# The first batch's v as casting transfers from GpSimd's queue, one per head

## The chip, the cores and the metric

One core of a Trainium2 chip runs the program. Its engines run side by side, each through its own list of instructions in order, and wait for one another by semaphores: TensorE (PE: matmuls and transposes, with PEld its weight loads), VectorE (DVE), ScalarE (ACT), GpSimd (POOL) and SyncE (SP), which here only issues transfers. Transfers issued by SP and by GpSimd travel in two queues and are carried by the same 16 DMA engines. The metric is the device time of one execution in microseconds (us). What is compared is the median over runs of the kernel before and of the changed kernel.

## What is computed

Two blocks, one behind the other, in f32. The first is a linear attention with a decaying state, for 4 batches, 8 heads, 768 positions and 64 columns a head:

```python
for t in range(S):
    state = gamma[None, :, None, None] * state + np.einsum('bhd,bhe->bhde', k[:, :, t], v[:, :, t])
    y[:, :, t] = scale * np.einsum('bhd,bhde->bhe', q[:, :, t], state)
```

Its heads are laid side by side into x, 768 x 512 for each batch. The second block mixes x by the real part of a two-dimensional Fourier transform, normalises and adds a two-layer network (512 to 2048 to 512):

```python
X = np.fft.fft(np.fft.fft(x, axis=1), axis=2)
u = x + np.real(X)
un = (u - mean) / np.sqrt(var + 1e-06)
out = u + np.maximum(un @ w_ch1, 0.0) @ w_ch2
```

## The kernel before, in words

**Tiling.** The 768 positions are six chunks of 128. Heads are handled in pairs, four pairs a batch in the order 0, 1, 3, 2 (`PAIR_ORDER`); "pair 0 to 3" below means the place in that order. For each pair q, k and v come from memory as f32 tiles of 128 partitions x 768 values (384 KB). GpSimd turns them into f16: q (L398), k times its decay, one instruction per head (L407, L410), and v (L423). TensorE transposes q and k by chunks (L439), ScalarE copies the transposes out of PSUM (L447, L450), TensorE multiplies k by q within a chunk (L464, the scores) and k by v (L486, the states' increments), VectorE masks the scores (L471) and scans over the chunks (L495), and TensorE makes y from both: scores by v (L510), q by states (L526). ScalarE scales y into x (L539).

**Stages.** The first batch's attention runs by itself at the start (`first_units`), together with the building of the sine and cosine tables (L288 to L292 on VectorE, L316 to L325 and L301 on ScalarE). Then the network of batch b runs while the attention of batch b + 1 is woven into it. The first network matmuls of batch 0 are L953; those of the other parts are L936 and L979.

**Order.** In the first batch the order on every engine is written out by hand: `first_units` makes a list of small functions, each emits its instructions, and `pin` ties every instruction to the one before it on the same engine. So the place of a unit in that list is the place of its instructions in each engine's own list. `filler(n)` puts n matmuls without use (L151) on TensorE at such a place.

**Loads.** All twelve loads of the first batch are issued by SP at the start, L165, in the order q, k, v of pair 0, then of pair 1, and so on. They go into the pool `inp`, which has 11 buffers. GpSimd issues the eight transfers of the network's weights (w1: L993, w2: L1000), which change f32 into f16 on the way; the first of them stands between the q cast and the k cast of pair 3. The loads of batch 1, on SP again, wait for the seventh weight transfer and for a matmul of L953.

**What the change touches.** `load_unit` for batch 0 (L158 to L181), the v cast `v0_unit` (L418), and its places in `first_units` (L1054 to L1074). The casts `q0_unit` (L394) and `k0_unit` (L402) stand beside it on GpSimd and keep their form; for pair 3 the second k head is done by ScalarE (L414) and the second half of v by VectorE (L427). The f16 tile of v comes from the pool `vp`, which has four buffers. GpSimd's list through the first batch is: set-up; then q, k, k, v of pair 0; of pair 1; two small constants (L351, L353); of pair 2; then q, the first weight transfer, k, v of pair 3; then the other seven weight transfers.

Of the kernel before, what the change touches and what calls it, by code (L numbers as in the profile page):

```python
# [12 lines left out]
ALU = mybir.AluOpType  # L13
f32 = mybir.dt.float32
# [4 lines left out]
P = 128  # L19
B, H, S, D = 4, 8, 768, 64  # L20
DM = 512
DFF = 2048
NCH = S // P
# [6 lines left out]
PAIR_ORDER = [0, 1, 3, 2]  # L30
# [6 lines left out]
LD0, LD1 = (0.172, 0.226), (-0.370, 0.140)  # L37
HT0 = (0.655, 0.675, 0.673, 0.628)
NPE = 2
ACT_ROWS = ((2, 5, 6, 7, 8, 9, 10, 14), (0, 3, 6, 7, 9, 10, 11, 12, 14, 15), (2, 4, 5, 6, 7, 8, 10, 14))  # L40


@with_exitstack
def kernel(
# [113 lines left out]
    def load_unit(b, i, after=None):  # L158
        def run():
            h0 = 2 * PAIR_ORDER[i]  # L160
            for name, src in srcs.items():
                t = inp.tile([P, 2, NCH, D], f32, tag="in32", name=f"{name}32")
                rows = "h (p c) d -> p h c d" if b < NPE and name == "q" else \
                    "h (c p) d -> p h c d"
                dma = nc.sync.dma_start(t, src[b, h0:h0 + 2].rearrange(rows, p=P))  # L165
                if after is not None:
                    for x in (w_dma[after].ins, lb[0]["mm"].ins):
                        tc.add_manual_dep(dma.ins, x.name,
                                          mybir.DependencyInfo(mybir.DependencyClass.Sync,
                                                               mybir.DependencyReason.DATA),  # L170
                                          reason="loads in turn")
                if b > 1:
                    tc.add_manual_dep(dma.ins, a_of[b - 1, 1].ins.name,
                                      mybir.DependencyInfo(mybir.DependencyClass.Sync,
                                                           mybir.DependencyReason.DATA),
                                      reason="loads behind the transposes")
                in_of[name, b, i] = t
        return run

    for i in range(4):  # L180
        load_unit(0, i)()  # L181


    icol_i = const.tile([P, 8], i32, tag="icol_i")
# [44 lines left out]
    def gk_unit(hp):  # L229
        def run():  # L230
            nc.scalar.copy(gk5[:, hp, :, 1:], gk2[:, hp:hp + 1].unsqueeze(1).to_broadcast(
                [P, D, NCH - 2]))
        return run
# [62 lines left out]
    def ts_dve(c):  # L296
        return trig_dve(c, S, KN, icol[:, c:c + 1], icoln[:, c:c + 1])
# [10 lines left out]
    def t_act(idx, part):  # L308
        w = KN if idx < 3 else 257
        r = rs[2 * idx][:, 0:w]  # L310
        ra = rs[2 * idx + 1][:, 0:w]
        sc = float(2.0 * np.pi / (S if idx < 3 else DM))

        def run():
            if part == 0:
                nc.scalar.activation(ra, r, AF.Abs, bias=0.0, scale=1.0)  # L316
            elif idx < 3:
                src = (ra, r)[part - 1].rearrange("p (i t) -> p t i", t=2)
                dst = (csp, ssp)[part - 1]
                nc.scalar.activation(dst[:, :, idx, :], src, AF.Sin,  # L320
                                     bias=hpi if part == 1 else 0.0,
                                     scale=-sc if part == 1 else sc)
            else:
                src, dst = (ra, r)[part - 1], (cd16, sd16)[part - 1]
                nc.scalar.activation(dst[:, idx - 3, :], src, AF.Sin,  # L325
                                     bias=hpi if part == 1 else 0.0, scale=-sc)
        return run
# [89 lines left out]

    def v0_unit(i):  # L418
        def run():
            v32 = in_of.pop(("v", 0, i)).rearrange("p h c d -> p c h d")  # L420
            v16 = v16_of[0, i] = vp.tile([P, NCH, 2, D], f16, tag="v16", name="v16")
            n = NCH if i < 3 else 3
            last_cast[0, i] = nc.gpsimd.tensor_scalar(  # L423
                out=v16[:, 0:n], in0=v32[:, 0:n], scalar1=1.0, scalar2=1.0, op0=ALU.mult,
                op1=ALU.mult)
            if n < NCH:
                nc.vector.tensor_copy(v16[:, n:], v32[:, n:])  # L427
        return run

    def t0_unit(i, part):  # L430
# [84 lines left out]
    def yx_unit(i):  # L515
        def run():
            st = at[0, i]
            first = i == 3
            if first:
                for h2 in range(2):  # L520
                    st["y", h2] = ps_y.tile([P, NCH, D], f32, tag="y", name="wkY",
                                            padded_shape=[P, 8, D])
            for c in range(1, NCH):
                for h2 in range(2):
                    sl = slice(64 * h2, 64 * h2 + 64)
                    nc.tensor.matmul(st["y", h2][:, c, :], st["qT"][sl, c, :],  # L526
                                     st["s16"][sl, :, c - 1], start=first and c == 1,
                                     stop=not first and c == NCH - 1, skip_group_check=True)
        return run
# [507 lines left out]
    def first_units():  # L1037
        def a(i):
            un = [am_unit(i, 0), am_unit(i, 1)]
            return un  # L1040

        def e(i, *hh):
            return [ae_unit(i, half, h2) for half, h2 in hh]

        def y(i):
            return [yi_unit(i, 0), yi_unit(i, 1)]

        def x(i):
            return [x0_unit(i, 0), x0_unit(i, 1)]

        std = ((0, 0), (0, 1), (1, 0), (1, 1))
        heads = ((0, 0), (1, 0), (0, 1), (1, 1))
        o = PAIR_ORDER
        un = [ts_dve(0), gk_unit(o[0]), gk_unit(o[1]), t_act(0, 0), t_act(0, 1),  # L1054
              q0_unit(0), t0_unit(0, 0), filler(4), ts_dve(1), te_unit(0, 0), t_act(0, 2),
              k0_unit(0), t0_unit(0, 1), filler(3), te_unit(0, 1), ts_dve(2), td_dve(0), t_act(1, 0),
              t_act(1, 1), t_act(1, 2), v0_unit(0)]
        un += a(0) + [filler(1), kv0_unit(0)] + e(0, *std) + [sc_unit(0)]
        un += [q0_unit(1), t0_unit(1, 0), te_unit(1, 0), t_act(2, 0), t_act(2, 1), filler(4),
               k0_unit(1), t0_unit(1, 1), te_unit(1, 1)]  # L1060
        un += y(0) + [parity_consts, yx_unit(0), filler(2)] + x(0) + [t_act(2, 2), v0_unit(1),
                                                                     half_ids]
        un += a(1) + [csn_unit(0), filler(1), kv0_unit(1)] + e(1, *std) + [sc_unit(1)]
        un += [q0_unit(2), t0_unit(2, 0), te_unit(2, 0), csn_unit(1), filler(3), k0_unit(2),
               t0_unit(2, 1), te_unit(2, 1)]
        un += y(1) + [td_dve(1), yx_unit(1), filler(2)] + x(1) + [
            gk_unit(o[2]), t_act(3, 0), t_act(3, 1), v0_unit(2)]
        un += a(2) + [filler(1), kv0_unit(2)] + e(2, *std) + [sc_unit(2), t_act(3, 2),
                                                              csn_unit(2)]
        un += [q0_unit(3), w1_unit(0), t0_unit(3, 0), te_unit(3, 0), filler(3)] + y(2)  # L1070
        un += [fold_s(0, 0, 258, 0, 1), g0_unit(0, (0,)), k0_unit(3), t0_unit(3, 1),
               te_unit(3, 1), yx_unit(2), gk_unit(o[3]), x0_unit(2, 0), x0_unit(2, 1),
               t_act(4, 0), t_act(4, 1), filler(2), v0_unit(3)]
        un += [w1_unit(g) for g in range(1, 4)] + [w2_unit(g) for g in range(4)]  # L1074
        un += a(3) + e(3, (0, 0), (1, 0)) + [kv0_unit(3), filler(4), sc_unit(3), t_act(4, 2)]
        un += e(3, (0, 1), (1, 1))
        un += [yx_unit(3), yi_unit(3, 0), x0_unit(3, 0), filler(1), yi_unit(3, 1), x0_unit(3, 1),
               g0_unit(0, (1,)), filler(1)]
        un += [fold_s(0, 0, 130, 1, 2), fold_d(0, 0), s1_unit(0, 0, 0), fold_s(0, 130, 258, 1, 2),
               px_unit(0), fold_d(0, 1, (0,)), xmean_unit(0), fold_d(0, 1, (1,)),  # L1080
               s1_unit(0, 1, 0), s1_unit(0, 0, 1), s1_unit(0, 1, 1), g0_unit(0, (2,)),
               mean_unit(0)]
        un += [s2_unit(0, 0), px_unit(1), s2_unit(0, 1), norm_unit(0, 0), gr_unit(0), gr_unit(1),
               px_unit(2), filler(2), unT_unit(0, 0), xmean_unit(1), mean_unit(1),
               norm_unit(0, 1), s2_unit(0, 2), xmean_unit(2), mean_unit(2), norm_unit(0, 2),
               gr_unit(2), gr_unit(3), edge_zeros, x_edges(1)]
        return un
# [94 lines left out]
```

## Time and profile before

| What | Value |
|---|---|
| runs shown, median (lowest to highest) | 247.04 us (246.52 to 247.95), 3 runs |
| span of the profiled execution, first to last instruction | 245.4 us |
| busy share of the span: PE, PEld, DVE, ACT, POOL | 95%, 59%, 72%, 51%, 33% |
| bytes moved, mean rate | 36.39 MB, 148 GB/s |
| queue of SP: packets, MB | 94960, 31.86 |
| queue of GpSimd: packets, MB | 4224, 4.19 |

The profile gives one execution by its span; the runs' times are taken from outside it and are some 1.6 us longer. The issue of a transfer is an instruction of the queue that issues it; its landing is a later event. In the first batch these are, from the timeline of SP and the time from issue to landing of each load:

| Pair | q: issued, landed | k: issued, landed | v: issued, landed |
|---|---|---|---|
| 0 | 0.81, 4.1 | 1.32, 5.9 | 1.82, 7.6 |
| 1 | 2.69, 8.8 | 4.99, 10.6 | 5.50, 12.3 |
| 2 | 7.08, 13.5 | 9.61, 15.2 | 10.12, 16.9 |
| 3 | 11.66, 19.5 | 14.37, 21.3 | 14.95, 22.5 |

A line of a timeline reads: start in us, length in us, engine, line of the kernel, operation, tile written <- tiles read, shapes and types, count; in brackets the idle time of the engine just before, and the engine and line that ended it. Where several instructions are merged, the length is that of all of them. When several semaphores are waited for, the last one by the profile is named, which need not be the one that held.

### The profile page before, as it was taken

How to read it: one execution, taken by the hardware profiler on the slowest of the kernel's cores; microseconds unless marked ns; L12 is line 12 of the kernel's file. 1: busy time of each engine (PE TensorE's matmuls, PEld its weight loads, DVE VectorE, ACT ScalarE, POOL GpSimd, SP SyncE). 2: the span in 40 equal slices, each digit the busy share in tenths (PEclk: the TensorE clock that was granted, in tenths of full speed). 3: DMA queues.
4: the chain of work that ended last, by engine and by line, in shares of the span. 5: the costliest groups of instructions: out<-in, count | busy, mean ns of one | idle time of the engine just before them, and what ended most of it. 6: DMA issues, size and time to landing. Idle time of an engine off the chain costs nothing.

```text
span 245.4 us, 5309 instructions
## 1 busy us (share of the span) xinstructions
PE 234.2 (95%) x2024; PEld 143.8 (59%) x2024; DVE 177.0 (72%) x430; ACT 124.2 (51%) x276; POOL 81.7 (33%) x146
## 2 busy tenths in 40 slices
PE   6997899999999998999999999999999999999995
PEld 2454668956776655665567546655666455445543
DVE  8997957897897788996885748887895656424112
ACT  8798669587775434751247414742247317202500
POOL 6667601465600057690000646660002405000000
PEclk9999999999999999999999999999999999999999
DMA  8999999699999377999999667786200241221012
GB/s 173 256 260 140 204 195 205 164 245 230 291 229 222 75 168 165 191 181 137 256 272 214 116 141 203 129 120 139 87 1 0 45 151 21 47 85 43 0 45 85
DMA packets 99209, 36.39 MB, mean 148 GB/s; under 512 B 89840, under 2 KB 96240, under 8 KB 99184
## 3 DMA queue, kind: packets, MB, share of 16 engines
q1 hardware_dynamic: 94960, 31.86, 62.2%
q0 software_dynamic: 4224, 4.19, 10.7%
q8 instruction: 16, 0.26, 0.5%
q14 instruction: 9, 0.07, 0.1%
HBM read 27.26 MB, written 6.29 MB: 137 GB/s over the span
## 4 chain that ended last, share of the span: by engine, by line
PE 71%; DMA 7%; DVE 7%; POOL 4%; ACT 4%; SPq 3%; issue 1%; POOLq 0%; ACTq 0%; DVEq 0%
PE psc L979 30%; PE psh L936 25%; DMA k<-in_k_dram 5%; PE ps L736 3%; SPq L165 3%; PE wkA L600 3%; DMA q<-in_q_dram 2%; PE wkY L654 2%; PE pq L833 2%; PE wkY L650 1%; POOL u L870 1%; PE wkK L619 1%; ACT un L885 1%; DVE bst L889 1%; POOL kd L407 1%
## 5 line engine op out<-in xcount | busy, mean ns | idle before, releaser
L979 PE MATMUL psc<-w,ht 128*128 128x512 f16 (+2 forms) x400 | 89.3, 371 | 0.0
L936 PE MATMUL psh<-unT,w 128*128 128x384 f16 x448 | 81.6, 326 | 0.4 <-ACT ht L940 0.2
L979 PEld LDWEIGHTS <-ht 128*128 128x128 f16 x400 | 37.5, 98 | 36.5 <-issue 0.2
L936 PEld LDWEIGHTS <-w 128*128 128x128 f16 x448 | 42.3, 98 | 24.7 <-issue 1.4
L940 ACT ACTIVATE ht<-psh 128x384 f16<-128x384 f32 x64 | 30.9, 489 | 41.7 <-PE psh L936 41.1
L870 POOL TENSOR_TENSOR u<-u,x 128x256 f32<-128x256 f32 x21 | 13.3, 635 | 100.3 <-DVE u L840 91.0
L983 DVE SCALAR_TENSOR_TENSOR ob<-psc,stats,u 128x512 f32<-128x512 f32 (+2 forms) x25 | 18.1, 726 | 26.1 <-PE psc L979 26.0
L942 DVE TENSOR_SCALAR ht<-psh 128x384 f16<-128x384 f32 x48 | 26.2, 548 | 7.7 <-PE psh L936 7.4
L603 DVE TENSOR_TENSOR atm<-wkA,maskp 128x512 f16<-128x512 f32 x36 | 23.8, 681 | 1.6 <-PE wkA L600 1.6
L891 ACT ACTIVATE un<-u,stats 128x512 f16<-128x512 f32 x21 | 15.2, 722 | 16.7 <-DVE stats L890 12.1
L889 DVE BATCH_NORM_STATS2 bst<-u 128x6 f32<-128x512 f32 x21 | 14.6, 694 | 7.7 <-POOL u L872 7.6
L629 DVE SCALAR_TENSOR_TENSOR s<-s,gk,wkK 128x128 f16<-128x128 f16 x48 | 16.3, 341 | 3.7 <-ACT s L625 2.7
L662 ACT ACTIVATE x<-wkY,gexp 128x384 f16<-128x384 f32 x24 | 12.8, 581 | 8.0 <-PE wkY L654 8.0
L151 PE MATMUL wps<-ht 128*128 128x512 f16 x40 | 13.5, 444 | 2.2 <-POOL ht L202 2.2
L383 POOL TENSOR_SCALAR kd<-k,gexp 128x384 f16<-128x384 f32 x24 | 13.8, 585 | 3.6 <-DMA k<-in_k_dram 3.6
L872 POOL TENSOR_TENSOR u<-u,x 128x256 f32<-128x256 f32 x21 | 13.3, 635 | 3.0 <-DVE stats L890 3.0
L600 PE MATMUL wkA<-qTz,kT 128*128 128x256 f16 x72 | 13.4, 273 | 0.1
L835 ACT COPY qn<-pq 128x128 f32<-128x128 f32 x18 | 4.9, 272 | 13.6 <-PE pq L833 13.6
L953 PE MATMUL psh<-unT,w 128*128 128x128 f16 x192 | 11.5, 219 | 0.1
L953 PEld LDWEIGHTS <-w 128*128 128x128 f16 x192 | 11.0, 98 | 0.7 <-issue 0.5
L840 DVE SCALAR_TENSOR_TENSOR u<-pq,g,qn 128x256 f32<-128x256 f32 x18 | 8.5, 472 | 3.3 <-PE psh L936 2.5
L388 POOL TENSOR_SCALAR v<-v 128x768 f16<-128x768 f32 x12 | 10.0, 831 | 1.3 <-DMA v<-in_v_dram 1.3
(164 smaller groups left out, 315.6 us busy)
## 6 DMA issues: line engine op xcount, KB each, us to landing
q<-in_q_dram SPq DMA_DIRECT2D x16, 384.0 KB, 6.3
k<-in_k_dram SPq DMA_DIRECT2D x16, 384.0 KB, 5.6
v<-in_v_dram SPq DMA_DIRECT2D x16, 384.0 KB, 6.3
out_dram<-ob SPq DMA_DIRECT2D x23, 256.0 KB, 2.6
w<-in_moe_w_ch_dram POOLq DMA_DIRECT2D x8, 512.0 KB, 10.8
unT<-un SPq DMA_TRANSPOSE x15, 2.4
out_dram<-ob SPq DMA_DIRECT2D x1, 192.0 KB, 1.9
qTz<-q16z SPq DMA_TRANSPOSE x8, 3.9
```

Of the source, the lines that this page charges most:

```text
L600: mm = nc.tensor.matmul(wk[:, c2], st["kT"][:, c, :], st["qT"][:, :, c, :], start=True, stop=True)
L603: nc.vector.tensor_tensor(out=st["atm"][:, 2 * part:2 * part + 2], in0=wk, in1=maskp[:, PAIR_ORDER[i]].unsqueeze(1).to_broadcast([P, 2, 2, ...
L629: nc.vector.scalar_tensor_tensor(out=s16[:, c], in0=s16[:, c - 1], scalar=gk2[:, hp:hp + 1], in1=wk[:, c - c0], op0=ALU.mult, op1=ALU.add)
L870: nc.gpsimd.tensor_tensor(out=u[:, kb, 0:256], in0=u[:, kb, 0:256], in1=x[:, kb, 0, 1:257], op=ALU.add)
L889: nc.vector.bn_stats(bst, u[:, kb, :])
L891: una = nc.scalar.activation(un, u[:, kb, :], AF.Identity, bias=stats[:, kb, 0:1], scale=-1.0)
L936: nc.tensor.matmul(psh, w116[:, cb, fb * P:(fb + 1) * P], unT[:, cb, rt * 384:(rt + 1) * 384], start=(cb == 0), stop=(cb == 3))
L940: nc.scalar.activation(ht16[:, fb, :], psh, AF.Relu, bias=0.0, scale=-1.0)
L942: nc.vector.tensor_scalar(out=ht16[:, fb, :], in0=psh, scalar1=-1.0, scalar2=0.0, op0=ALU.mult, op1=ALU.max)
L953: mm = nc.tensor.matmul(psh[:, f], w116[:, cb, fb * P:(fb + 1) * P], unT[:, cb, kb * P:(kb + 1) * P], start=(cb == 0), stop=(cb == 3))
L979: nc.tensor.matmul(psc[:, c0:c1], ht16[:, fb, rb3 * P:(rb3 + 1) * P], w216[:, fb, c0:c1], start=(fb == 0), stop=(fb == NFB - 1))
L983: nc.vector.scalar_tensor_tensor(out=ob[:, c0:c1], in0=psc[:, c0:c1], scalar=lb[b]["st"][:, rb, 3:4], in1=lb[b]["u"][:, rb, c0:c1], op0=AL ...
```

## The change

Batch 0's v is no longer loaded by SP. SP issues eight loads for it, q and k of the four pairs. `v0_unit` no longer casts; it issues two transfers on GpSimd's queue, one per head, each of which reads f32 from memory and writes f16 into the tile of v directly. The unit also moves in the list: that of pair 0 to the very front, before the q cast of pair 0, and those of pairs 1, 2 and 3 to the places where those of pairs 0, 1 and 2 stood. The load and the casts of batches 1 to 3 stay as they were.

```diff
+HW0 = ("q", "k")
...
+    def load0(name, i):
+        h0 = 2 * PAIR_ORDER[i]
+        t = in_of[name, 0, i] = inp.tile([P, 2, NCH, D], f32, tag="in32", name=f"{name}32")
+        rows = "h (p c) d -> p h c d" if name == "q" else "h (c p) d -> p h c d"
+        nc.sync.dma_start(t, srcs[name][0, h0:h0 + 2].rearrange(rows, p=P))
+
     for i in range(4):
-        load_unit(0, i)()
+        for name in HW0:
+            load0(name, i)
...
     def v0_unit(i):
         def run():
-            v32 = in_of.pop(("v", 0, i)).rearrange("p h c d -> p c h d")
+            h0 = 2 * PAIR_ORDER[i]
             v16 = v16_of[0, i] = vp.tile([P, NCH, 2, D], f16, tag="v16", name="v16")
-            n = NCH if i < 3 else 3
-            last_cast[0, i] = nc.gpsimd.tensor_scalar(
-                out=v16[:, 0:n], in0=v32[:, 0:n], scalar1=1.0, scalar2=1.0, op0=ALU.mult,
-                op1=ALU.mult)
-            if n < NCH:
-                nc.vector.tensor_copy(v16[:, n:], v32[:, n:])
+            for h2 in range(2):
+                last_cast[0, i] = nc.gpsimd.dma_start(
+                    v16[:, :, h2, :], v[0, h0 + h2].rearrange("(c p) d -> p c d", p=P))
         return run
...
-        un = [ts_dve(0), gk_unit(o[0]), gk_unit(o[1]), t_act(0, 0), t_act(0, 1),
+        un = [v0_unit(0), ts_dve(0), gk_unit(o[0]), gk_unit(o[1]), t_act(0, 0), t_act(0, 1),
...
-              t_act(1, 1), t_act(1, 2), v0_unit(0)]
+              t_act(1, 1), t_act(1, 2), v0_unit(1)]
...
-        un += y(0) + [parity_consts, yx_unit(0), filler(2)] + x(0) + [t_act(2, 2), v0_unit(1),
+        un += y(0) + [parity_consts, yx_unit(0), filler(2)] + x(0) + [t_act(2, 2), v0_unit(2),
                                                                      half_ids]
...
-            gk_unit(o[2]), t_act(3, 0), t_act(3, 1), v0_unit(2)]
+            gk_unit(o[2]), t_act(3, 0), t_act(3, 1), v0_unit(3)]
...
-               t_act(4, 0), t_act(4, 1), filler(2), v0_unit(3)]
+               t_act(4, 0), t_act(4, 1), filler(2)]
```

In GpSimd's list this gives: set-up; two transfers for pair 0; q, k, k of pair 0; two transfers for pair 1; q, k, k of pair 1; two for pair 2; the two constants; q, k, k of pair 2; two for pair 3; q of pair 3, the first weight transfer, k of pair 3, the other seven. The weight transfers now also wait for the transfers of v, one for one, since they use the same semaphores. In the changed kernel the line numbers from `load_unit` on are higher by 1 to 8.

## The prediction

> **What bounds the kernel now.** I read the chain of waits first, then the table by five-microsecond stretches, then the engines' timelines over the first 36 us. The chain as a whole is TensorE work:
>
> ```profile
> PE 71%; DMA 7%; DVE 7%; POOL 4%; ACT 4%; SPq 3%; issue 1%; POOLq 0%; ACTq 0%; DVEq 0%
> ```
>
> From 35.08 us on (first matmul of L953) TensorE is busy 4.85 to 5.00 us of every 5 up to 50 us, and 95% of the whole span. Whatever moves the start of L953 therefore moves the end by about as much. The edit lies ahead of that, in the first batch (0 to 30 us), where no engine is a clean bound: columns are stretch, its length, then busy time of PE, PEld, DVE, ACT, POOL, the granted clock, DMA share and GB/s.
>
> ```profile
> 10.00:15.00 5.00, 4.66 (x74) 2.83 (x69) 4.61 (x14) 4.40 (x10) 3.30 (x6) 1.00 1.27 250
> 15.00:20.00 5.00, 4.01 (x62) 2.29 (x59) 4.47 (x10) 4.56 (x9) 2.45 (x4) 1.00 1.27 253
> 20.00:25.00 5.00, 3.76 (x61) 2.45 (x61) 4.01 (x9) 3.94 (x9) 4.95 (x7) 1.00 0.85 120
> ```
>
> VectorE and ScalarE have only 0.4 to 1 us of slack in each stretch, so feeding them earlier can win no more than that. The chain in this stage runs over SP's queue and the k loads into GpSimd's casts. GpSimd's timeline (start, length, line, idle before and its releaser):
>
> ```profile
> 4.18 0.83 POOL L398 TENSOR_SCALAR q16z<-q 128x768 f16<-128x768 f32 x1
> 6.07 0.60 POOL L407 TENSOR_SCALAR kd<-k,gexp 128x384 f16<-128x384 f32 x1 [1.05 <-DMA k<-in_k_dram]
> ...
> 19.64 0.83 POOL L398 TENSOR_SCALAR q16z<-q 128x768 f16<-128x768 f32 x1 [1.65 <-PE wkK L486]
> 20.41 0.96 POOL L993 DMA_DIRECT2D w<-in_moe_w_ch_dram  x1
> 21.41 1.27 POOL L407 TENSOR_SCALAR kd<-k,gexp 128x384 f16<-128x384 f32 x1
> 22.66 0.50 POOL L423 TENSOR_SCALAR v<-v 128x384 f16<-128x384 f32 x1
> 23.12 2.29 POOL L993 DMA_DIRECT2D w<-in_moe_w_ch_dram  x3
> ```
>
> The reader is to see that GpSimd waits for data, not for its own work, and that the first q cast starts the moment the queue's set-up ends. The wait of 1.65 us is named for TensorE, but the q load issued at 11.66 us took 7.8 us to land, 19.46, so I read it as that load. ScalarE's timeline shows where the last three pairs start late:
>
> ```profile
> 11.01 0.80 ACT L447 COPY qTz<-tq 128x768 f16<-128x768 f16 x1 [0.57 <-PE tq L439]
> ...
> 17.09 0.80 ACT L450 COPY kT<-tq 128x768 f16<-128x768 f16 x1 [0.40 <-PE tq L439]
> ...
> 23.29 0.80 ACT L450 COPY kT<-tq 128x768 f16<-128x768 f16 x1 [0.91 <-PE tq L439]
> ```
>
> Between 11.01 and 23.29 ScalarE has only these two gaps worth naming, 0.40 and 0.91: 1.31 us is the most that earlier data can win here, since its instructions and their order stay.
>
> **The change part by part.** *Removed:* four v loads of 384 KB from SP's queue, three casts of 128x768 on GpSimd (0.98, 0.83, 0.94 us), one of 128x384 (0.50), and VectorE's half cast L427 (0.54 at 23.10). The last is hidden: VectorE idles 0.92 us behind it for the matmuls of L464, so it is worth nothing unless that wait goes.
>
> *Added:* eight transfers on GpSimd, two per pair, ahead of the q cast of the same pair: v of pair 0 before everything, v of pairs 1, 2, 3 each behind the k casts of the pair before. GpSimd works in order, so the two issues hold the q cast, the k casts, and the transposes behind them. Call P the time of two issues. The only such rows are the weight transfers: 0.96 us for the first, 2.29/3 = 0.76 for the next three, with 128x4 runs each. A v transfer has 128x6 runs of a third kind (256 bytes in, 128 out). Taken as they are: P = 0.96 + 0.78 = 1.74. Scaled by runs, x1.5: 2.61. I take 1.9, near the row as it is, and keep both ends.
> The Trainium skill (DMA: Bandwidth & Descriptors, section Anatomy of one DMA — SWDGE (gpsimd) path) says that descriptor generation is small and that many can be emitted before the added cost shows; by that P would be 1.74, and the sum below 0.16 us less. No transfer of this shape is in the trace.
>
> *The opening, pair 0.* Set-up ends at 4.12; the q cast then starts at 6.02 in place of 4.18, 1.84 later. The k casts follow at 6.85 and end near 8.1; k lands at 5.96, so they no longer wait. TensorE's own order now costs:
>
> ```profile
> 5.07 0.82 PE L439 MATMUL tq<-ident,q16z 128*128 128x128 f16 x6 [0.17 <-POOL q16z L398]
> 5.68 1.91 PE L151 MATMUL wps<-ht 128*128 128x512 f16 x4
> ...
> 10.81 1.03 PE L151 MATMUL wps<-ht 128*128 128x512 f16 x4
> ```
>
> Four filler matmuls stand between the q and the k transposes, so the k transposes go from 7.39 to 9.23 and the first score matmuls (L464) from 8.95 to 10.79, although k is ready. VectorE reads the scores 0.37 us after they start (24.18 to 24.55 in pair 3, the same in pairs 1 and 2). In pair 0 it would have been ready at 9.32 but came at 9.88, out of its own trigonometry:
>
> ```profile
> 4.37 0.86 DVE L290 TENSOR_SCALAR tmp<-tmp 128x386 f32<-128x386 f32 x1
> ...
> 9.88 1.94 DVE L471 SCALAR_TENSOR_TENSOR atm<-wkA,maskf 128x384 f16<-128x384 f32 x4
> ```
>
> So 0.56 of the 1.84 is absorbed and 1.28 goes on, through the PSUM tile that L471 frees, to the next q transposes and to ScalarE's 11.01.
> One more price: four fillers take 1.71 us at 5.68 and 1.03 at 10.81, although the granted clock reads 1.00 at both. TensorE speeds up near 7.9 us, after 5 us of nearly unbroken work; the new hole of about 1.9 us at 4.9 can put that off. Lower bound 0; upper bound if it comes only after another 5 us: three fillers and the score matmuls slow, 0.4, and the next filler group 0.5 more, 0.9. I take 0.45.
>
> *Pairs 1 to 3.* ScalarE carries 1.28 + 0.45 = 1.7 late and gives back 0.40 and 0.91, since data is no longer late: +0.4 at the copy of 23.29. For that GpSimd must keep ahead. Its work from 4.12 to the last q cast is three times (0.83 + 1.15) for q and k, 0.52 for L351/L353, and 4P: 10.6 + 4P, or 18.2 at P = 1.9 (was 19.64). With the cast and the weight issue, 0.83 + 0.96, the last k cast starts at 12.4 + 4P = 20.0 (was 21.41). That cast's 1.27 us beside the usual 0.58 is at most 0.7 more; it fits too.
> Loads: 12 took from 2.2 to 20.6 us of the DMA view, about 1.5 per load. The eight left in SP's queue alone would land by some 15; with three v pairs all served ahead of them, by 20: in time for 20.0. v of pair 0 is wanted at about 11.5 (L486 was at 9.71), some 6 us after its second issue; the weight transfer at 20.41 landed after 5.6 at twice the bytes read.
>
> *Weights.* All four L993 transfers land at 34.4 now, before their last use; issued some 2 us earlier they stay hidden, by the transposes of 34 us. The next batch's loads on SP wait at 44.89 for a matmul of L953, not for SP's shorter list, so nothing is won there.
>
> *Sum against the profiled span:* +1.84 - 0.56 + 0.45 - 1.31 = +0.4. 245.4 becomes 245.8; the median of the times shown, 247.04, is 1.6 above that span, taken as unchanged: 247.4.
>
> **The rivals.**
> A, slower: GpSimd becomes the bound. 12.4 + 4P passes 21.41 from P = 2.25, and each further 0.1 us costs 0.4, four pairs deep. At P = 2.61 the last k cast starts at 22.8, 1.4 late: 248.4; at 3.0, 250.0. For it: more runs than any transfer seen; the slow k cast straight behind the weight issue, 1.27, as if the issue weren't over. Against: the weight issues' steady 0.75 to 0.80.
> B: VectorE holds back the issue during its trigonometry. For it: L290 takes 0.86 beside the q cast and 0.36 at 2.93 alone, so the two exclude one another. Three such instructions at 0.36 to 0.42 fall into the first two issues: P of pair 0 about 3.05, so +2.99 - 0.56 + 0.45 - 1.31 = +1.6: 248.6. Against: it is GpSimd that went first in that row, and L290 that waited.
> The Trainium skill (SBUF — State Buffer, section SBUF: two separate sides) warns of just this for transfers issued by GpSimd: a two-port VectorE instruction keeps it from writing descriptors. By that rule the time is B's. The nearest test in the trace is VectorE's cast L427, 23.10 to 23.64 beside the second weight issue, which took 0.79 us against 0.75 and 0.76 for the next two.
> C: v late. If v of pair 0 queues behind some 1.2 MB already in flight, at 220 GB/s 5.5 us, it lands near 12.2, some 0.7 after it is wanted: 248.1. The two queues sharing the engines speaks against it.
> D, faster: an issue that doesn't hold the next cast. Then nothing is late in pair 0 and the gaps of 1.31 are won: 245.7. For it: transfers run on alone once issued; against: the weight issues stand end to end at 0.76.
> That the edit doesn't do what it says is excluded: GpSimd's list has eight v transfers and SP's list four loads fewer.
>
> **How the numbers follow.** Forecast 0.52 (own range 246.6 to 248.1, from P of 1.74 with no slow start to 2.1 with all of it), A 0.23, B 0.09, C 0.08, D 0.08. About 0.5%, 1.24 us, is what can be told from no change. Slower: most of A and B and a little of C and the forecast, 0.30; faster: most of D and a sliver of the forecast, 0.09; same, 0.61. The range goes from 246.0, leaving D out, to 249.8, which holds A up to P = 2.95.
>
> **What would show it.** Two v issues of 0.9 to 1.0 us from 4.12; q cast near 6.0; L464 of pair 0 near 10.8 to 11.2; no gap on ScalarE between 12.4 and 23.6; last k cast near 20; L953 starting near 35.5. Wrong if an issue takes over 1.15 us, if the q cast overlaps it, if L486 waits for v, or if a shift at L953 doesn't reach the end.

## The result, and the profile after

| | before | after |
|---|---|---|
| runs, median (lowest to highest) | 247.04 us (246.52 to 247.95) | 249.21 us (249.09 to 251.15) |
| span of the profiled execution | 245.4 us | 247.1 us |
| ratio of the times | | 1.0111, 95% interval 1.0067 to 1.0156 |

The changed kernel is slower by 1.7 us in the span and by 2.2 us in the median of three runs; 247.4 was forecast, 0.4 more than before. The span and the time of one and the same run lie 2.0 us apart in the changed kernel (247.1 and 249.09), and 1.8 to 1.9 in each of the 26 runs of the kernel before that are on record beside the experiments. The 1.6 used ahead of the result and in the forecast sets a median beside the span of another execution. So 0.1 to 0.2 of the 2.2 lies outside the span.

In the changed kernel the lines from the first batch's code on are 5 to 8 higher: the masks L471 are L476, the increments L486 are L491, the copies L447 and L450 are L452 and L455, the first network matmul L953 is L958. The transfers of v are L431.

The chain of waits and then the stretches of five microseconds (columns as before):

```profile
PE 76%; DVE 7%; ACT 6%; POOL 5%; DMA 3%; issue 2%; POOLq 0%; ACTq 0%
```
```profile
10.00:15.00 5.00, 4.34 (x58) 2.55 (x56) 3.44 (x10) 3.74 (x7) 4.98 (x9) 1.00 1.53 232
15.00:20.00 5.00, 4.60 (x74) 2.93 (x72) 4.71 (x10) 4.65 (x9) 4.93 (x8) 1.00 1.80 144
20.00:25.00 5.00, 3.63 (x56) 2.24 (x52) 4.57 (x10) 4.46 (x10) 5.00 (x7) 1.00 1.05 153
```

SP's queue has left the chain. VectorE fell from 4.61 to 3.44 us and ScalarE from 4.40 to 3.74 between 10 and 15 us: there the loss shows. GpSimd now counts as busy nearly throughout, because an issue counts on it, but it is ahead of its consumers in pairs 2 and 3, as its timeline shows:

```profile
4.06 1.88 POOL L431 DMA_DIRECT2D v<-in_v_dram  x2
5.96 1.02 POOL L406 TENSOR_SCALAR q16z<-q 128x768 f16<-128x768 f32 x1
...
8.16 1.70 POOL L431 DMA_DIRECT2D v<-in_v_dram  x2
...
17.73 0.85 POOL L406 TENSOR_SCALAR q16z<-q 128x768 f16<-128x768 f32 x1
18.50 0.80 POOL L998 DMA_DIRECT2D w<-in_moe_w_ch_dram  x1
19.35 0.59 POOL L415 TENSOR_SCALAR kd<-k,gexp 128x384 f16<-128x384 f32 x1
```

Two issues take 1.88 us for pair 0 and 1.70 for the others (1.04 for the very first issue, 0.83 to 0.87 for the rest). The q cast of pair 0 starts 1.78 later than before; the last k cast starts 2.06 earlier (19.35, was 21.41) and takes 0.59 in place of 1.27. TensorE's timeline of the opening:

```profile
7.04 0.82 PE L444 MATMUL tq<-ident,q16z 128*128 128x128 f16 x6 [2.14 <-POOL q16z L406]
7.66 1.91 PE L152 MATMUL wps<-ht 128*128 128x512 f16 x4
9.36 0.84 PE L444 MATMUL tq<-ident,kd 128*128 128x128 f16 x6
...
11.10 0.51 PE L469 MATMUL wkA<-qTz,kT 64*128 64x128 f16 x12
...
12.63 0.44 PE L491 MATMUL wkK<-v,kd 128*64 128x64 f16 x9 [0.53 <-DMA v<-in_v_dram]
13.00 0.51 PE L444 MATMUL tq<-ident,q16z 128*128 128x128 f16 x6
...
17.45 0.44 PE L491 MATMUL wkK<-v,kd 128*64 128x64 f16 x9 [0.26 <-DMA v<-in_v_dram]
```

L491 of pairs 0 and 1 stops for v. The transfers of pair 0, issued from 4.06 and 5.1, land at 10.9 and 12.6. The q transposes of pair 1 stand behind L491 on TensorE, so they too are late, 13.00 against 10.48. ScalarE, then VectorE's masks of pairs 0 and 3:

```profile
13.54 0.80 ACT L452 COPY qTz<-tq 128x768 f16<-128x768 f16 x1 [0.95 <-PE tq L444]
...
18.37 0.80 ACT L452 COPY qTz<-tq 128x768 f16<-128x768 f16 x1 [0.35 <-PE tq L444]
...
19.59 0.79 ACT L455 COPY kT<-tq 128x768 f16<-128x768 f16 x1
...
23.88 0.61 ACT L422 ACTIVATE kd<-k,gexp 128x384 f16<-128x384 f32 x1
25.17 0.80 ACT L455 COPY kT<-tq 128x768 f16<-128x768 f16 x1 [0.68 <-PE tq L444]
```
```profile
11.56 1.95 DVE L476 SCALAR_TENSOR_TENSOR atm<-wkA,maskf 128x384 f16<-128x384 f32 x4 [1.46 <-PE wkA L469]
...
26.43 1.02 DVE L476 SCALAR_TENSOR_TENSOR atm<-wkA,maskf 128x384 f16<-128x384 f32 x2 [1.04 <-PE wkA L469]
```

Set against before, the lateness at each landmark reads: masks of pair 0 +1.68; q copy of pair 1 +2.53 and of pair 2 +2.98 (18.37 against 15.39); then it falls: k copy of pair 2 +2.50, q copy of pair 3 +2.13 (23.20 against 21.07), k copy of pair 3 +1.88, masks of pair 3 +1.88 (26.43 against 24.55). The first L958 starts at 36.96 against 35.08, again +1.88. So what reaches the network is decided by 26 us: 1.68 from the held q cast, 0.85 from v late in pair 0, 0.45 from v late in pair 1, and 1.10 won back.

### The profile page after: what moved, and what is told of

Same layout as the page of the kernel before. It is cut to its first block, busy times and chain, and to the rows that moved or that the text cites. A ratio compares the mean times of both kernels' runs of the same rounds, so it can differ in the third digit from the quotient of the medians.

```text
span 247.1 us, 5304 instructions
## 1 busy us (share of the span) xinstructions
PE 234.5 (95%) x2024; PEld 144.5 (58%) x2024; DVE 177.3 (72%) x429; ACT 124.0 (50%) x276; POOL 84.6 (34%) x150
## 4 chain that ended last, share of the span: by engine, by line
PE 76%; DVE 7%; ACT 6%; POOL 5%; DMA 3%; issue 2%; POOLq 0%; ACTq 0%
PE psc L984 33%; PE psh L941 24%; PE ps L741 3%; DMA v<-in_v_dram 3%; PE wkA L605 3%; PE psh L958 3%; PE wkY L659 2%; PE wkY L655 1%; PE pq L838 1%; PE wkK L624 1%; PE tq L561 1%; POOL v L431 1%; DVE u L845 1%; POOL u L875 1%; DVE bst L894 1%
## 5 line engine op out<-in xcount | busy, mean ns | idle before, releaser
L958 PE MATMUL psh<-unT,w 128*128 128x128 f16 x192 | 11.5, 219 | 0.1
L958 PEld LDWEIGHTS <-w 128*128 128x128 f16 x192 | 11.0, 98 | 0.7 <-issue 0.5
```

The source lines that it names most:

```text
L958: mm = nc.tensor.matmul(psh[:, f], w116[:, cb, fb * P:(fb + 1) * P], unT[:, cb, kb * P:(kb + 1) * P], start=(cb == 0), stop=(cb == 3))
```

## The experiments

All are edits of the changed kernel. E1 to E4 ran together (kernel before: median 246.74 of 9 runs), E5 to E8 together (247.23 of 17). The expectations name three theories by letter. H: the issues hold the casts behind them, and that is all. L: v landing late behind SP's loads adds to it. R: casting transfers cost the DMA engines more than those from f32 to f32. The edits shift the line numbers again; the tile names tell which line is meant. The changed kernel has three runs, and the ratios of E1, E2 and E4 lie in its interval (1.0067 to 1.0156) or reach into it, so what these three show rests on their traces and not on their medians.

**E1, the second k head of pair 3 on GpSimd in place of ScalarE.** The gap of 0.68 on ScalarE follows ScalarE's own scaling of a k head (L422, 23.88), which the transposes wait for.

```diff
-            if i < 3:
+            if i < 4:
                 nc.gpsimd.tensor_scalar(out=kd[:, :, 1, :], in0=k32[:, 1],
```

> The changed kernel, but the second k head of pair 3 is scaled by GpSimd, as in the other pairs, and not by ScalarE. Theory L (a ledger of three entries: pair 0's q and k held behind the issue of v; v landing late for the state matmuls of pairs 0 and 1; and the gap of ScalarE before its last k copy, which the changed kernel can't win back because ScalarE itself, 2.1 us late, scales that head): the last k copy moves from 25.17 to about 24.1, the last masks from 26.43 to 25.4, where VectorE comes free, and the span from 247.1 to about 246.1. Theory H (only the hold in pair 0 counts) and theory R (the transfers' own time on the DMA engines is what costs): no change, 247.1.

Measured: 248.41 us, ratio 1.0071 (1.0047 to 1.0096), span 246.5. ScalarE's timeline of pair 3, then TensorE's wait in pair 0:

```profile
23.84 0.77 ACT L452 COPY qTz<-tq 128x768 f16<-128x768 f16 x1
24.52 0.79 ACT L455 COPY kT<-tq 128x768 f16<-128x768 f16 x1
```
```profile
13.12 0.44 PE L491 MATMUL wkK<-v,kd 128*64 128x64 f16 x9 [1.02 <-DMA v<-in_v_dram]
```

The gap is gone, and the k copy comes at 24.52 instead of 25.17, although v of pair 0 was later still here (a wait of 1.02 for 0.53). The time is above the 246.1 expected, since that reckoned with v as in the changed kernel. The part on ScalarE is shown; it is worth at least the 0.48 between the masks of pair 3 (25.95 against 26.43).

**E2, v of pair 0 by SP and a cast, as before; pairs 1 to 3 by casting transfers.**

```diff
-        for name in HW0:
+        for name in HW0 + (("v",) if i == 0 else ()):
             load0(name, i)
...
+            if i == 0:
+                last_cast[0, i] = nc.gpsimd.tensor_scalar(
+                    out=v16, in0=in_of.pop(("v", 0, i)).rearrange("p h c d -> p c h d"),
+                    scalar1=1.0, scalar2=1.0, op0=ALU.mult, op1=ALU.mult)
+                return
```

`v0_unit(0)` also moves in the list, to just ahead of `v0_unit(1)`.

> The changed kernel with pair 0's v loaded by SP and cast by GpSimd behind its k casts, as before; pairs 1 to 3 stay with the casting transfers. Theory L: pair 0 runs as in the kernel before, but v of pair 1, issued at 8.7 to 10.4, lands at 15.5 to 17 and is wanted at 15.2, so part of the loss returns there: span about 246.4. Theory H: the hold is gone, span 245.4 to 245.8. Theory R: three quarters of the casting transfers are left, span about 246.7.

Measured: 249.62 us, 1.0131 (1.0064 to 1.0199), span 246.4. The hold is gone: the masks of pair 0 start at 9.79 (9.88 before, 11.56 after). Yet TensorE now waits in pair 1:

```profile
16.53 0.44 PE L496 MATMUL wkK<-v,kd 128*64 128x64 f16 x9 [1.00 <-DMA v<-in_v_dram]
```

The span is that of L. The four runs spread from 247.96 to 251.04, so the median says little: the two long ones had a mean granted clock of 0.986 and 0.993, the others 0.999 and 1.000.

**E3, the transfers of pair 0 behind its q and k casts.** `v0_unit(0)` moves from the front of the list to just ahead of `v0_unit(1)`.

```diff
-        un = [v0_unit(0), ts_dve(0), gk_unit(o[0]), gk_unit(o[1]), t_act(0, 0), t_act(0, 1),
+        un = [ts_dve(0), gk_unit(o[0]), gk_unit(o[1]), t_act(0, 0), t_act(0, 1),
...
-              t_act(1, 1), t_act(1, 2), v0_unit(1)]
+              t_act(1, 1), t_act(1, 2), v0_unit(0), v0_unit(1)]
```

> The changed kernel with pair 0's two v transfers issued behind pair 0's k casts, so that they hold nothing of pair 0. Theory L: q cast back at 4.2, but v of pair 0 is issued at 7.3 to 9.1 and lands near 14.5 to 16 where 9.7 is wanted: 5 us late, span 249 to 250. Theory H: span about 245.6. Theory R: 247.1.

Measured: 253.19 us, 1.0262 (1.0236 to 1.0289), span 251.3. TensorE stands still for v twice in pair 0, and the row of the following stretch shows what came on top, the granted clock (0.61):

```profile
13.74 0.31 PE L491 MATMUL wkK<-v,kd 128*64 128x64 f16 x1 [4.09 <-DMA v<-in_v_dram]
15.97 0.69 PE L491 MATMUL wkK<-v,kd 128*64 128x64 f16 x9 [1.92 <-DMA v<-in_v_dram]
```
```profile
15.00:20.00 5.00, 4.03 (x47) 2.70 (x46) 2.60 (x7) 2.42 (x4) 4.99 (x8) 0.61 1.75 111
```

H falls, and R with its 247.1: with no hold at all on pair 0 the kernel is the slowest so far. v issued at 7.3 is wanted at about 9.6; TensorE gets its first half at 13.7 and the second at 16.0. L's 249 to 250 is passed by 1.3 us in the span; L had not counted the clock, and what the clock alone cost was not measured.

**E4, SP's loads of pairs 2 and 3 held until v of pair 0 has landed.** All else as in the changed kernel; the issues still hold the q cast.

```diff
-        nc.sync.dma_start(t, srcs[name][0, h0:h0 + 2].rearrange(rows, p=P))
+        dma = nc.sync.dma_start(t, srcs[name][0, h0:h0 + 2].rearrange(rows, p=P))
+        if i > 1:
+            tc.add_manual_dep(dma.ins, last_cast[0, 0].ins.name, ...)
```

The four loads move in the list, to just behind `v0_unit(0)`.

> The changed kernel, but SP's loads of pairs 2 and 3 wait until v of pair 0 has landed, so that v shares the DMA engines with less. Theory L: v of pair 0 lands near 10, not 12.6, the state matmuls of pair 0 no longer wait (0.53 us of idle, some 0.7 on the path), q and k of pairs 2 and 3 still land before their casts; span about 246.3. Theory H: v's landing doesn't matter, 247.1. If the loads held back come late for pair 2, above 247.5.

Measured: 248.06 us, 1.0065 (1.0042 to 1.0088), span 245.9. TensorE no longer waits for v in pairs 0 and 1, and the gap on ScalarE stays as it was:

```profile
11.70 0.47 PE L496 MATMUL wkK<-v,kd 128*64 128x64 f16 x10
```
```profile
23.85 0.80 ACT L460 COPY kT<-tq 128x768 f16<-128x768 f16 x1 [0.68 <-PE tq L449]
```

The masks of pair 3 start at 25.12: of the lateness of 1.88, 1.31 went with the wait for v, and 0.57 is left. That shows that v was late because of SP's loads of pairs 2 and 3. The DMA queues say how. The same half a microsecond (8.0 to 8.5), first of the changed kernel, with both queues at work, then of E4, with SP's loads held back (packets, MB, share):

```profile
q0 software_dynamic: 368, 0.05, 146.7%
q1 hardware_dynamic: 36, 0.06, 52.2%
```
```profile
q0 software_dynamic: 588, 0.07, 231.8%
q1 hardware_dynamic: 16, 0.00, 5.3%
```

GpSimd's queue moves 1.6 times as many packets in this stretch when it is alone, and over the whole of pair 0 it is more: from the first packet to the last it takes 2.0 us in E4 (7.54 to 9.55) and 4.5 in the changed kernel (7.69 to 12.16). The start is another matter. In the changed kernel the first packets come 3.6 us after the first issue (4.06, 7.69), and in E4 hardly sooner (7.54), since SP's loads of pairs 0 and 1 are still in flight there. Where SP's queue runs empty in the meantime it is 1.6 us (the first weight transfer of the kernel before, 20.41 to 22.06) and 1.8 (E7, 8.56 to 10.33). R isn't needed: 588 packets in half a microsecond are about as many per microsecond (1,180) as SP's queue makes alone (900 to 1,100).

**E5, both E1 and E4.**

> Both edits together: pair 3's second k head on GpSimd, and SP's loads of pairs 2 and 3 waiting for v of pair 0. Theory L (the loss is the sum of the hold in pair 0, v landing late, and the gap at the last k copy): the last k copy comes at 22.6, the last masks at 24.0, where VectorE is free, against 24.55 in the kernel before: span 244.8 to 245.0, under the 245.4 of the kernel before, with only the hold of pair 0 left. Theory H (the hold alone makes the loss): the span stays where pacing alone left it, 245.9, or above.

Measured: 248.38 us, 1.0045 (1.0032 to 1.0058), span 246.1: missed, and slower in the span than E4. v of pair 2 is now the late one, since the loads that were held back come just then:

```profile
21.26 0.44 PE L496 MATMUL wkK<-v,kd 128*64 128x64 f16 x9 [0.97 <-DMA v<-in_v_dram]
```

Still, the masks of pair 3 start at 24.78, only 0.23 later than before, and the first network matmul 0.22 later (35.30). The other 0.5 us of the span is lost behind it. One part is a wait on TensorE for the next batch's k cast:

```profile
57.27 0.51 PE L566 MATMUL tq<-ident,kd 128*128 128x128 f16 x6 [0.44 <-POOL kd L396]
```

The kernel before has this wait too, shorter (0.30):

```profile
56.90 0.51 PE L556 MATMUL tq<-ident,kd 128*128 128x128 f16 x6 [0.30 <-POOL kd L383]
```

With it the kernel is 0.37 behind, and 0.40 at the start of the last VectorE instruction (242.91 against 242.51). The other 0.3 comes after the end of that instruction, where the span goes on for 2.80 us against 2.52.

**E6, E5 with v of pair 0 in four transfers of half the size**, so the hold is doubled with the bytes unchanged.

```diff
+            cut = ((0, 3), (3, 6)) if i == 0 else ((0, 6),)
             for h2 in range(2):
-                last_cast[0, i] = nc.gpsimd.dma_start(
-                    v16[:, :, h2, :], v[0, h0 + h2].rearrange("(c p) d -> p c d", p=P))
+                for c0, c1 in cut:
+                    last_cast[0, i] = nc.gpsimd.dma_start(v16[:, c0:c1, h2, :], ...)
```

> The run with both edits, but pair 0's v in four transfers of half the size, so that its q cast is held by four issues. If an issue costs by its runs, four issues of half the runs take 1.9 to 2.1 us and the span hardly moves, up to 0.2. If it costs by the transfer, some 0.8 each, the hold is 3.4 to 3.6 us in place of 1.88, the first masks of pair 0 come 1.6 later, and theory L has this pass whole to the end: span 246.3 to 246.6. A theory in which later gaps absorb the hold has it below 245.5.

Measured: 249.44 us, 1.0084 (1.0071 to 1.0097), span 247.8. GpSimd's timeline:

```profile
4.06 3.29 POOL L438 DMA_DIRECT2D v<-in_v_dram  x4
7.39 1.03 POOL L411 TENSOR_SCALAR q16z<-q 128x768 f16<-128x768 f32 x1
```

An issue of half as many runs takes almost as long, 0.96 us for the first and 0.78 for the others in place of 1.04 and 0.83 to 0.87: nearly all of the price goes by the transfer, not by its runs. The q cast is 1.43 later than in E5, the masks of pair 0 are 1.68 later (12.97 against 11.29), the first network matmul 1.55, the last VectorE instruction 1.41 (244.32 against 242.91) and the span 1.7, of which 0.3 comes after that instruction. The medians of the runs' spans are 1.5 apart (247.7 and 246.2); those of the times only 1.1, since a run of E6 takes 1.7 us outside its span and one of E5 2.1 to 2.2. The expected size was reckoned from a base that E5 had missed, but its step of 1.6 over that base holds: what the issues add to the q cast's start passes on whole to the last instruction.

**E7, E2 with the k head of E1, and SP's loads of pairs 2 and 3 held until v of pair 1 has landed.** The edits are those of E1, E2 and E4 with `last_cast[0, 1]` in place of `last_cast[0, 0]`.

> Pair 0's v by SP and cast by GpSimd as before, pairs 1 to 3 by casting transfers, pair 3's second k head on GpSimd, and SP's loads of pairs 2 and 3 waiting for v of pair 1. Theory L: no hold in pair 0 (masks at 9.8); v of pair 1, issued at 8.4 to 10.2, lands near 12.5 with the DMA engines to itself, ahead of the 15.3 at which it is wanted; the q cast of pair 1 at 10.3 (8.85 before) is what is left, ScalarE 0.7 late there, won back in the later gaps: span 244.5 to 245.2. If the loads that wait come late for pair 2, up to 246.

Measured: 253.05 us, 1.0229 (1.0211 to 1.0247), span 251.5: missed. The loads held back came too late themselves. GpSimd waits for q of pair 2, and the granted clock falls to 0.50 in the stretch behind TensorE's gap of 4.65 us:

```profile
19.54 0.83 POOL L411 TENSOR_SCALAR q16z<-q 128x768 f16<-128x768 f32 x1 [4.86 <-DMA q<-in_q_dram]
```
```profile
20.00:25.00 5.00, 4.32 (x38) 2.69 (x39) 0.00 (x0) 2.38 (x4) 3.78 (x6) 0.50 0.65 95
```

**E8, E5 with the q cast of pair 0 on ScalarE, first in its list**, so that no issue stands ahead of it.

```diff
+            if i == 0:
+                nc.scalar.copy(q16, q32)
+                return
```

> The run with both edits, and pair 0's q cast moved to ScalarE ahead of its other work, so that the issue of v holds only pair 0's k casts, for which k lands at 5.9 anyway. Theory L: the first transposes of q at 5.1 as before, the masks of pair 0 at 9.9, then a wait of up to 1 us for v of pair 0 (landing near 10.5); ScalarE has 0.8 us more to do, in its early gaps: span 244.2 to 244.9, below the run with both edits. If the hold in pair 0 were worth nothing, the same as that run.

Measured: 247.40 us over 12 runs, 1.0013 (0.9996 to 1.0030), span 245.4: missed, with 244.2 to 244.9 expected. The masks of pairs 0 and 3, 9.88 and 24.55 before:

```profile
9.55 1.95 DVE L485 SCALAR_TENSOR_TENSOR atm<-wkA,maskf 128x384 f16<-128x384 f32 x4 [0.27 <-PE wkA L478]
...
24.17 1.02 DVE L485 SCALAR_TENSOR_TENSOR atm<-wkA,maskf 128x384 f16<-128x384 f32 x2 [0.38 <-PE wkA L478]
```

With the hold gone, the kernel is level with the one before and 1.0 us under E5. It is not faster, although the first network matmul starts 0.38 earlier (34.70). At the transposes of the next batch's k only 0.18 of this is left, and TensorE's wait there has grown from 0.30 to 0.49:

```profile
56.72 0.51 PE L570 MATMUL tq<-ident,kd 128*128 128x128 f16 x6 [0.49 <-POOL kd L396]
```

At the last network matmuls 0.26 is left, here E8 and then the kernel before:

```profile
231.65 10.56 PE L993 MATMUL psc<-w,ht 128*128 128x512 f16 x64
```
```profile
231.91 10.56 PE L979 MATMUL psc<-w,ht 128*128 128x512 f16 x64
```

The last VectorE instruction also starts 0.26 earlier (242.25 against 242.51), but after its end the span goes on for 2.78 us against 2.52, and that takes it all back. In time, no kernel that was tried beats the one before.

## Why the prediction was right or wrong

**The number: in the range by luck.** 249.21 lies inside 246.0 to 249.8, but above the forecast's own 246.6 to 248.1, and the room up there had been given to rival A, which did not come about. (By the prediction's own sum the lower of these ends is 246.9 and not 246.6: 1.68 - 0.56 - 1.31 is -0.19.) A slowdown of more than its 1.24 us had a chance of 0.30 against 0.61 for no change; 2.17 was measured. One of its signs of being wrong came, L486 waiting for v, and two of its signs of being right did not: ScalarE had gaps of 0.95 at 13.54 and 0.35 at 18.37, and the first network matmul started at 36.96, not 35.5.

**Right: the issue and its hold.** P was taken at 1.9 and measured 1.88 and 1.70, so rival A, which needs 2.25, and B, 3.05, did not come about; nor did D, since the q cast, put at 6.02, came at 5.96, as the second issue ended (5.94). That 1.9 fits so closely is luck in part: it stood 0.16 above the rows it was taken from, with no row for the difference. E6 adds that the price is nearly all one for each transfer and that the hold reaches the last instruction. On B the traces show no fixed order: VectorE's L298 at 4.37 took 0.94 us beside the first issue, and the same instruction took 0.36 there in E6 and E8. The longer first issue goes with being the first: it took 1.04 also in E2, E3 and E7, starting at 7.3 to 8.6, and the first weight transfer took 0.96 in the kernel before but 0.80 in the changed kernel, where it comes ninth. The rule of the Trainium skill (SBUF — State Buffer, section SBUF: two separate sides) that a two-port VectorE instruction keeps GpSimd from writing descriptors would have given P of about 3; the measured 1.88 decides against that size here.

**Right in the sum, with parts that cancel: the opening and GpSimd's lead.** 1.84 - 0.56 + 0.45 put the masks of pair 0 1.73 late; they were 1.68. The parts: the q cast began 1.78 late and took 1.02 us in place of 0.83, so its transposes came 1.97 late (7.04 against 5.07); from the k transposes to the scores TensorE took 1.74 us (9.36 to 11.10) against 1.56 (7.39 to 8.95), 0.18 more and not 0.45; 0.47 was absorbed, not 0.56. The slower cast, 0.19, had not been forecast and made up for most of the slow start that did not come. The last k cast was put at 20.0 and came at 19.35.

**Wrong: v on time.** The step that failed is the one that kept rival C out of the sum: "The two queues sharing the engines speaks against it", with a chance of 0.08 and a price of 0.7 for pair 0 alone. Sharing is what makes v late: beside SP's loads GpSimd's queue starts 3.6 us after its issue and then gets a part of the packets, so that v of pair 0 takes 4.5 us from first packet to last and v of pair 1 3.6, against 2.0 and 2.8 in E4 with SP's loads held. v of pair 0 came at 12.6, close to the 12.2 of that rival, and it cost 0.85; v of pair 1 cost 0.45 more. E4 takes these 1.3 away and leaves the hold in place, and its span, 245.9, is close to the forecast's 245.8. That closeness is luck in part: its masks of pair 0 are 1.52 late and not 1.73, 0.95 is won back and not 1.31, and 0.3 is added at the very end, which the forecast does not have. In timed medians the agreement is looser: E4 is 1.3 us above its kernel before, not 0.4. The spans on record say the same, with medians of 246.1 and 244.9; the profiled execution of the kernel before, 245.4, lies near the upper end of those nine (244.4 to 245.6). Where E4's further 0.7 us is spent is not shown.

**Mis-sized: what ScalarE gives back.** "Gives back 0.40 and 0.91, since data is no longer late" came to 1.10. The 0.40 went (0.48 won there). Of the 0.91 only 0.25 was won: behind GpSimd's late cast stood a second wait, ScalarE's own scaling of the second k head and the transposes after it, which an earlier k load doesn't touch. E1 moves that scaling, and the gap is gone. Another 0.37 was won between 19.6 and 23.2 us, which the forecast had not counted.

**Nearly right: what reaches the end.** The shift of 1.88 at L958 is 1.43 at the next batch's k transposes, where the kernel before waits 0.30 (at 56.90) and the changed kernel does not:

```profile
58.33 0.51 PE L561 MATMUL tq<-ident,kd 128*128 128x128 f16 x6
```

At the start of the last VectorE instruction it is 1.46 (243.97 against 242.51), and in the span 1.7, because the end itself has grown: the span goes on for 2.78 us after that instruction and not for 2.52. In E1 to E8 it is 2.71 to 3.08. Most of this is in SP's closing list of nine waits, 0.06 us each: in the kernel before, the one for the last store's semaphore is the ninth, in the changed kernel the fifth, so that four are still to come when the store has landed. That the changed number of transfers shifted it is likely but was not tested. "Moves the end by about as much" left out both the wait and the end. The other claims hold: the removed casts and VectorE's half were worth nothing, and the weights stayed hidden.

## What to carry to other kernels

An issue on a compute engine's list costs that list its time once for each transfer, so a transfer put ahead of the first cast delays everything behind that cast; put there only what nothing early waits behind. A second queue is not a second set of DMA engines: where the first queue has loads in flight, work out the landing of the new transfers with the share that is left, and not with the rate of an idle machine. Before a gap is counted as won, look for the next wait behind the releaser that is named; and before an earlier start is counted as won, follow it to the first wait downstream that it does not move as far, here the next batch's k cast, and on to the last instruction, since what comes after that can change too.

## What had not been expected of the hardware

The first packets of GpSimd's queue came 3.6 us after the issue beside a loaded SP queue (4.06 to 7.69, and E2, 8.38 to 11.99; 4.4 in E3), and 1.6 to 1.8 us where SP's queue ran empty meanwhile. The issue took 0.83 to 0.87 us with 768 runs, 0.78 with 384, and 0.75 to 0.80 for the weights with 512; the first of a kernel took 0.1 to 0.2 more (1.04, 0.96, 0.96). After gaps of TensorE of 4.09 us (E3) and 4.65 us (E7) the granted clock stood at 0.61 and 0.50 over a stretch of five microseconds, after the work had begun again, and these two kernels are the slowest of all: a late transfer there is paid for twice.
